# The output sums of an attention's last head group laid out anew over its slots, and wo's range maxima pinned into the filter's first loop

## The chip, the cores and the metric

The kernel runs on one core of a Trainium2 chip. The metric is the device time of one execution in microseconds (us), as the median of several runs; lower is better. Alongside it stands a profile: one execution recorded by the hardware, with the start and end of every instruction on each engine. PE is the matrix engine (TensorE), DVE the vector engine, ACT the scalar engine, POOL the general engine (GpSimd), SP the engine that issues the transfers (DMA). All times are in us unless ns stands beside them. L443 means line 443 of the kernel before.

## The reference, cut to what matters

Two layers, each an attention block and then a spectral filter, on x of 2048 x 1024 in float32:

```python
x = A_x
x = x + _A_ref(_layernorm(x, axis=-1), A_wqkv, A_wo)   # 32 heads of 32, softmax, output times wo
x = x + _B_ref(_layernorm(x, axis=-1), B_w_r, B_w_i)   # rfft2, times w, irfft2
x = x + _A_ref(_layernorm(x, axis=-1), A_wqkv, A_wo)
x = x + _B_ref(_layernorm(x, axis=-1), B_w_r, B_w_i)
return x
```

The end of `_A_ref` is what the change moves: the heads' outputs o (2048 x 1024), times wo (1024 x 1024), added to x.

## The kernel before

**Attention.** The 32 heads are worked in eight head groups of four (g = 0 to 7). A group runs over four chunks of 512 queries (c) and sixteen tiles of 128 keys (kt), so 64 steps u. A step computes the scores of one key tile for four heads (`S`, L558: twelve matmuls on a quarter of the array each) into two score buffers of two PSUM banks, and ACT turns each of them into p by an exponential (L562). Every second step PE multiplies the p of the two steps before with V (`PV`, L568), and DVE adds p into two running sums (`add`, L579 and L581, one add of 128 x 1024 for each buffer), from which the softmax's divisor comes at the end of a chunk (`fin`, L587 to L594); `out` (L600, L601) then makes the normalised head outputs as two float16 parts. There are three score buffers (`psS`), used in turn; L587's sums and the rests (below) take one of the same three.

**Slots.** After every odd step the order of PE's work, which is written out by hand (PE and ACT keep the order of the program in this part), has a slot for other matmuls: u // 2 counts them, 32 in a group. In groups 0 to 6 they hold the next group's projections. The output product is done in the slots at the end of group 6 and in those of group 7.

**The output product.** It goes by 12 tiles t of 128 rows (chunks 0 to 2, four tiles each); the last chunk's four tiles come after the slots, in the tail (`first`, `last`, `whole`). A tile has two halves of 512 columns. The heads' outputs of groups 0 to 6 are read back from DRAM by `load_o(c)` (L432 to L435, two loads of 896 KB), into one of two places that chunks c and c + 2 share; those of group 7 are still in SBUF (`olast`) but are ready only some steps into the next chunk. So a tile has a **part** (`wo_part`, groups 0 to 6: 21 matmuls for each half, into the only bank `x`, then one evacuation on DVE that adds the residual `xres`, L466) and a **rest** (`wo_rest` and `wo_last`, group 7: 6 matmuls into a score buffer, L443, then on DVE the evacuation of 1024 columns, L475, the statistics for the next layer norm, L477 and L498, and a store to y, L478). `wo_part` is a generator that yields after each matmul; a slot takes so many steps of it.

In the slots of group 7 a slot takes either 21 steps (one half's part) or one rest. Tiles 2 and 3 have their parts in group 6; the 20 halves of 0, 1, 4 to 11 follow in that order, and rests go into every fourth step from the point on at which olast is there. `load_o(2)` comes after tile 1, `load_o(3)` after tile 7.

**The planner.** On the engines whose order isn't written out (DVE, POOL and SP in attention, all engines elsewhere) the framework orders the instructions by its own simulation: of those that are ready by its clock, the first in the program goes first. An instruction with its data early can so be issued far ahead of where the program has it. Each engine then takes its instructions strictly in the order that the planner wrote. Buffers are handed on when the last reader is done.

**The tail and the filter.** After the slots PE does the last chunk's tiles; meanwhile DVE and ACT normalise and fold the first twelve (`fold_rests`, L513 on ACT, L146 and L147 on DVE), which needs the statistics of all twelve (`mvs`). The filter then starts with a loop of 33 turns (`t1`, `fa`: transposes L791, matmuls L800, ACT's copies L96 and L804, DVE's subtraction L805), and a second loop over 32 units of the spectrum, whose weights w are loaded by `loadw` (L834). In layer 0 alone the first loop also takes the greatest magnitude of wo, for a check of the inputs' range that is read at the end: every odd turn loads a sixteenth of wo (L780, three buffers), and from the third on reduces one that was loaded before (`absmax`, L784, L785), the last three in one turn. The buffers of the first loop are freed at its end, and their memory is used again for the second's.

Of the kernel before, what the change touches and what calls it, by code (L numbers as in the profile page):

```python
# [6 lines left out]
F32 = mybir.dt.float32  # L7
# [5 lines left out]
ALU = mybir.AluOpType  # L13
AX = mybir.AxisListType
# [156 lines left out]
def run(g):  # L171
    for _ in g:
        pass
# [96 lines left out]
def attention(nc, tc, layer, ap, xin, yd, wts, wo, cst, dram, flags):  # L270
# [8 lines left out]
    sq, on, on2, sm = ap.sq, ap.on, ap.on2, ap.sm  # L279
# [5 lines left out]
    def bank():  # L285

        if both:
            both.append(True)
            if len(both) % 2:
                return psO.tile([128, 512], F32, name="o")  # L290
        return psX.tile([128, 512], F32, name="x")
# [104 lines left out]
    def sums(ph):  # L396
        return 8 if ph[0] == "v" else 4

    def filler():
        run(prep(phases[0]))  # L400
        for i, ph in enumerate(phases):
            nxt = prep(phases[i + 1]) if i + 1 < len(phases) else iter(())
            for n in range(sums(ph)):
                yield from (v_tiles if ph[0] == "v" else qk_chunk)(ph, n)
                for _ in range(1 + (n > 0)):
                    next(nxt, None)
            run(nxt)
# [6 lines left out]
    def load_wo():  # L414
        st = []

        def load(i):
            if i < 16:
                s = sgp.tile([128, 512], F32, name="wst")
                nc.sync.dma_start(s, wo[i // 2 * 128:i // 2 * 128 + 128, i % 2 * 512:i % 2 * 512 + 512])  # L420
                st.append(s)
        load(0)
        load(1)
        for i in range(16):
            load(i + 2)
            d, sl = i // 2, slice(i % 2 * 512, i % 2 * 512 + 512)
            split(nc, wo_t[0][d // 4][:, d % 4, sl], wo_t[1][d // 4][:, d % 4, sl], st[i], SW)
            yield
# [3 lines left out]
    def load_o(c):  # L432
        osb[c] = xhl[:, 2 + c % 2]
        for i in range(2):
            nc.sync.dma_start(osb[c][:, i, 0:7], od[i, 0:7, :, c * 512:(c + 1) * 512].rearrange("g p n -> p g n"))  # L435

    def wo_mm(p, c, t, n, ds, start=True, stop=True):

        for d in ds:
            oh, ol = ((olast[c][:, i] if d == 7 else osb[c][:, i, d])[:, t * 128:t * 128 + 128] for i in range(2))  # L440
            wh, wl = (wo_t[i][d // 4][:, d % 4, n * 512:n * 512 + 512] for i in range(2))
            for i, (a, b) in enumerate(((oh, wh), (oh, wl), (ol, wh))):
                nc.tensor.matmul(p, a, b, start=start and d == ds[0] and i == 0, stop=stop and d == ds[-1] and i == 2)  # L443
                yield

    def xres(c, t):
        if c == 3:
            x = pp.tile([128, 1024], F32, name="xres", tag="p")
        else:
            x = wqp.tile([128, 1024], F32, name="xres", tag="wqk")  # L450
        r0 = c * 512 + t * 128
        nc.sync.dma_start(x, xin[r0:r0 + 128, :])
        return x

    def wo_part(c, t, dst):

        x = xres(c, t)
        for n in range(2):
            p = bank()
            m = wo_mm(p, c, t, n, range(7))  # L460
            for _ in range(20):
                next(m)
                yield
            run(m)
            sl = slice(n * 512, n * 512 + 512)
            nc.vector.scalar_tensor_tensor(dst[:, sl], p, 1.0 / (SO * SW), x[:, sl], op0=ALU.mult, op1=ALU.add)  # L466
            yield

    def wo_last(c, t, p, src, y, start):

        for n in range(2):
            run(wo_mm(p[:, n], c, t, n, (7,), start=start))
        st = sm.tile([128, 2, 6], F32, name="st")
        r0 = c * 512 + t * 128
        nc.vector.scalar_tensor_tensor(y, p.rearrange("p n c -> p (n c)"), 1.0 / (SO * SW), src, op0=ALU.mult, op1=ALU.add)  # L475
        for n in range(2):
            nc.vector.bn_stats(st[:, n], y[:, n * 512:n * 512 + 512])  # L477
        nc.sync.dma_start(yd[r0:r0 + 128, :], y)  # L478
        return st

    wo_dst = [ap.x[:, 10 + t if t in SPILL else t] for t in range(8)] + [None] * 2 + [ap.x[:, t] for t in (10, 11)]

    def wo_parts():
        load_o(0)
        load_o(1)
        for t in [2, 3, 0, 1] + list(range(4, 12)):
            if t == 8:
                two = wvp.tile([128, 2, 1024], F32, name="wv")
                wo_dst[8], wo_dst[9] = two[:, 0], two[:, 1]
            yield from wo_part(t // 4, t % 4, wo_dst[t])  # L490
            if t in (1, 7):
                load_o(t // 4 + 2)

    mvs = sm.tile([128, 24], F32, name="mvs")

    def wo_rest(t):
        p = psS.tile([128, 2, 512], F32, name="s")
        nc.vector.bn_aggr(mvs[:, 2 * t:2 * t + 2], wo_last(t // 4, t % 4, p, wo_dst[t], wo_dst[t], True))  # L498
# [107 lines left out]

    pend, done, late = [], [], []
    fill, lwo, wof = filler(), load_wo(), wo_parts()
    left, parts, rests = 16, 20, list(range(12))

    def slots(f, sums, n, steps):

# [12 lines left out]
    with tc.manual_schedule(engines={mybir.EngineType.PE, mybir.EngineType.Activation}):  # L625
        for g in range(NG):
            todo = sum(sums(ph) for ph in beside.get(g, []))
            sl = slots(fill, todo, 22 if g == NG - 2 else 32, 24)
            wsl = slots(wof, 4, 10, 21)
            for u in range(NCH * NKT):  # L630
                c, kt = divmod(u, NKT)
                S(g, c, kt)
                if kt % 2 == 0:
                    for w in pend:
                        PV(*w)
                    late = pend
                    pend = []
                for w in late[:1]:
                    add(*w)
                    if w[2] == NKT - 1:  # L640
                        fin(*w[:2])
                        done = [w[:2]]
                late = late[1:]
                if kt == 5 and done:
                    out(*done.pop())
                pend.append((g, c, kt))
                if kt % 2 == 0:
                    continue
                if todo:
                    todo = next(sl)  # L650
                elif g == NG - 2:
                    if left:
                        run(lwo)
                        left = 0
                    if next(wsl, None) is not None and u == NCH * NKT - 1:
                        run(wsl)
                elif g == NG - 1:
                    t = rests[0] if rests else 16
                    if (t // 4 < c - 1 or t // 4 == c - 1 and kt >= 7) and (kt % 4 == 3 or not parts):
                        wo_rest(rests.pop(0))  # L660
                    elif parts:
                        parts -= 1
                        for _ in range(21):
                            next(wof)
                if g == NG - 2 and todo < 4:
                    for _ in range(2):
                        if left > (8 if todo == 3 else 0):
                            next(lwo, None)
                            left -= 1
        for w in pend:  # L670
            PV(*w)
        for w in late + pend:
            add(*w)
        run(wof)
        for t in rests:
            wo_rest(t)
    with tc.manual_schedule(engines={mybir.EngineType.PE}):
        ps, xs, folds = [], [xres(3, t) for t in range(4)], fold_rests()

# [70 lines left out]
def spectral(nc, tc, ap, yd, xout, a, cst, fast, flags=None, nxt=None):  # L750
# [7 lines left out]
    sfx, parts = ("_", 2) if fast else ("", 1)  # L758
# [15 lines left out]
    wos = []  # L774

    def absmax(i):

        if flags is not None and 0 <= i < 16:
            s = p3.tile([128, 512], F32, name="wo")
            nc.sync.dma_start(s, a["wo"][(i // 2) * 128:(i // 2 + 1) * 128, (i % 2) * 512:(i % 2) * 512 + 512])  # L780
            wos.append(s)
        while len(wos) == 3 or (wos and i == 15):
            m = p3.tile([128, 1], F32, name="wom")
            nc.vector.tensor_reduce(m, wos.pop(0), axis=AX.X, op=ALU.max, apply_absolute_value=True)  # L784
            nc.vector.tensor_max(flags["w"], flags["w"], m)  # L785

    def t1(i):
# [22 lines left out]
    for i in range(33):  # L810
        cur = t1(i) if i < 32 else None
        if prev is not None:
            fa(i - 1, prev)
        prev = cur
        if i % 2:
            absmax(i // 2)
# [127 lines left out]
    for i in range(36):  # L944
# [8 lines left out]
        if i % 2 and i < 32:  # L953
            t = i // 2
# [44 lines left out]
    for i in range(17):  # L999
        cur = [t2(i, g) for g in range(2)] if i < 16 else None  # L1000
        if prev is not None:
# [5 lines left out]
            elif i % 2 == 0:  # L1007
                sl = slice(i * 64 - 128, i * 64)
# [228 lines left out]
```

## Time and profile before

| | |
|---|---|
| median of 3 runs | 3907.49 us (3906.37 to 3912.81) |
| span of the profiled execution | 3906.3 us |
| its own time beside the span | none is listed |
| PE busy | 3737.0 us (96%) |
| DVE busy | 3181.5 us (81%) |
| ACT busy | 2899.6 us (74%) |
| POOL busy | 637.5 us (16%) |
| chain of work that ended last, by engine | PE 75%, DVE 10%, issue 7%, ACT 4% |

The views that the prediction reads: busy time by stretch (a row is the stretch, its length, then the busy time and number of instructions of PE, its weight loads, DVE, ACT and POOL, the granted clock of PE, the DMA engines' share and their GB/s); waits (who waited for whom: total us, times, longest); and the instructions in order of time (start, duration, engine, line, operation, tiles out<-in, shapes, how many were merged, and in brackets how long the engine had been idle and what ended it). Instructions overlap a little at their ends, so start to start says more of the pace than the durations do.

### The profile page before, as it was taken

The numbers are of one execution on the slowest core, as the hardware profiler recorded it, in microseconds if no ns is written. First come the engines' busy times: TensorE is split into PE (matmuls) and PEld (weight loads), VectorE is DVE, ScalarE is ACT, GpSimd is POOL, SyncE is SP. The second block draws the span as 40 slices with busy tenths as digits, with TensorE's granted clock in tenths as the row PEclk, the third lists the DMA queues.
The fourth block names the chain that finished last, engine by engine and source line by source line (L and its number), as shares of the span: only waits on it lengthen the run. The fifth ranks groups of instructions, "written<-read, shape, count | busy, mean of one in ns | idle before, by whom it ended". The sixth has DMA issues, their size and how long they took to land.

```text
span 3906.3 us, 79627 instructions
## 1 busy us (share of the span) xinstructions
PE 3737.0 (96%) x32951; PEld 1642.5 (42%) x32951; DVE 3181.5 (81%) x3793; ACT 2899.6 (74%) x3567; POOL 637.5 (16%) x560
## 2 busy tenths in 40 slices
PE   6999999999999999989989999999999999999998
PEld 4322432342234233368853334333423432333788
DVE  6689899889998987966665998889899888788554
ACT  4577787888788865657855888888888887666686
POOL 1111011101110200014321221122121102000143
PEclk9999999999999999999999999999999999999999
DMA  8000000000000221134170000000000002111333
GB/s 203 15 12 23 12 12 17 18 12 17 15 23 7 71 71 64 64 139 142 62 176 12 15 23 12 12 18 22 10 18 12 23 12 90 52 68 66 146 97 105
DMA packets 165573, 194.07 MB, mean 50 GB/s; under 512 B 74960, under 2 KB 120656, under 8 KB 164176
## 3 DMA queue, kind: packets, MB, share of 16 engines
q1 hardware_dynamic: 164912, 188.82, 15.2%
q8 instruction: 260, 4.26, 0.4%
q14 instruction: 113, 0.93, 0.1%
q10 hardware_dynamic: 288, 0.07, 0.0%
HBM read 123.83 MB, written 48.23 MB: 44 GB/s over the span
## 4 chain that ended last, share of the span: by engine, by line
PE 75%; DVE 10%; issue 7%; ACT 4%; DMA 2%; POOL 2%; SPq 0%; DVEq 0%; ACTq 0%; POOLq 0%
PE o L568 21%; PE s L558 17%; PE x L340 13%; PE x L384 7%; PE x L443 6%; ACT p L562 2%; DVE R L581 2%; PE ps L862 2%; PE ps L800 1%; PE s L587 1%; DMA w<-in_w 1%; PE ps L791 1%; PE s L443 1%; PE ps L977 1%; PE o L384 1%
## 5 line engine op out<-in xcount | busy, mean ns | idle before, releaser
L562 ACT ACTIVATE p<-s,bias 128x1024 f32<-128x1024 f32 x2048 | 2169.0, 1111 | 589.9 <-PE s L558 578.4
L581 DVE TENSOR_TENSOR R<-R,p 128x1024 f32<-128x1024 f32 x1792 | 2146.8, 1251 | 148.3 <-ACT p L562 144.2
L568 PE MATMUL o<-p,R 128*32 128x512 f32 x8192 | 986.1, 599 | 0.0
L340 PE MATMUL x<-big,wqk 128*128 128x512 f16 x2880 | 685.6, 384 | 21.9 <-DVE R L168 8.1
L558 PEld LDWEIGHTS <-R 32*128 32x128 f16 x12288 | 232.5, 92 | 780.2 <-issue 664.6
L340 PEld LDWEIGHTS <-wqk 128*128 128x128 f16 x3072 | 277.9, 98 | 460.1 <-issue 167.5
L558 PE MATMUL s<-R 32*128 32x512 f16 x6144 | 432.5, 379 | 19.1 <-ACT p L562 15.6
L558 PE MATMUL s<-Q,R 32*128 32x512 f16 x6144 | 433.0, 378 | 11.9 <-ACT p L562 10.6
L568 PEld LDWEIGHTS o<-p,R 128*32 128x32 f32 x8192 | 213.9, 109 | 525.6 <-issue 525.0
L601 POOL TENSOR_TENSOR ohl<-zt,ohl 128x512 f16<-128x512 f32 x62 | 180.3, 2907 | 1473.6 <-ACT ohl L600 1473.6
L384 PEld LDWEIGHTS <-big 128*128 128x128 f16 x3072 | 295.0, 99 | 159.7 <-issue 79.1
L384 PE MATMUL x<-wv,big 128*128 128x256 f16 x2688 | 323.2, 277 | 40.6 <-DMA big<-hl 34.6
L579 DVE SCALAR_TENSOR_TENSOR R<-p 128x1024 f32<-128x1024 f32 x128 | 153.9, 1204 | 198.7 <-ACT p L562 198.4
L344 POOL TENSOR_TENSOR sq<-R 128x512 bf16<-128x512 f16 x96 | 144.5, 1505 | 693.8 <-ACT R L167 690.6
L443 PE MATMUL x<-big 128*128 128x512 f16 x1050 | 237.4, 380 | 0.0
L443 PEld LDWEIGHTS <-big 128*128 128x128 f16 x1344 | 126.3, 98 | 177.3 <-issue 33.9
L910 DVE TENSOR_TENSOR H<-G,H 128x512 f16<-128x512 f32 (+1 forms) x68 | 46.9, 690 | 104.7 <-ACT H L909 104.6
L862 PE MATMUL ps<-cbi,H 128*128 128x256 f16 (+1 forms) x792 | 99.2, 273 | 5.6 <-ACT H L909 3.3
L855 ACT COPY U<-ps 64x256 f32<-64x256 f32 (+1 forms) x272 | 97.0, 357 | 8.5 <-PE ps L862 3.3
L855 ACT COPY B<-ps 64x256 f32<-64x256 f32 (+1 forms) x272 | 97.0, 356 | 6.7 <-PE ps L862 3.2
L344 POOL TENSOR_TENSOR sq<-Q 128x512 bf16<-128x512 f16 x32 | 44.6, 1395 | 319.7 <-ACT Q L167 319.7
L862 PE MATMUL ps<-cb,big 128*128 128x256 f16 x780 | 96.4, 273 | 0.0
(429 smaller groups left out, 3017.1 us busy)
## 6 DMA issues: line engine op xcount, KB each, us to landing
wst<-in_wp SPq DMA_DIRECT2D x96, 256.0 KB, 3.0
R<-y SPq DMA_DIRECT2D x32, 512.0 KB, 5.4
w<-in_w SPq DMA_DIRECT2D x60, 256.0 KB, 2.6
od<-ohl SPq DMA_DIRECT2D x56, 256.0 KB, 2.4
big<-od SPq DMA_DIRECT2D x16, 896.0 KB, 6.6
y<-R SPq DMA_DIRECT2D x20, 512.0 KB, 2.7
R<-in_x SPq DMA_DIRECT2D x16, 512.0 KB, 5.6
wst<-in_wo SPq DMA_DIRECT2D x32, 256.0 KB, 2.9
```

The costliest lines, as they stand in the source:

```text
L340: nc.tensor.matmul(ps, a, b, start=d == 0 and i == 0, stop=d == 7 and i == 2)
L344: nc.gpsimd.tensor_tensor(nrm[ph][:, c], t[:, 0], t[:, 0], op=ALU.mult)
L384: nc.tensor.matmul(ps[:, j], l, r, start=d == 0 and i == 0, stop=d == 7 and i == 2)
L443: nc.tensor.matmul(p, a, b, start=start and d == ds[0] and i == 0, stop=stop and d == ds[-1] and i == 2)
L558: nc.tensor.matmul(s[h // 2][:, h % 2], K[g][r, a, kt * 128:kt * 128 + 128], Q[g][r, b, c * 512:c * 512 + 512], start=i == 0, stop=i == 2)
L562: nc.scalar.activation(p, s[hf], AF.Exp, bias=bias[g], scale=SCALE / (SQ * SQ))
L568: nc.tensor.matmul(O[g, c][32 * h:32 * h + 32], V[g][:, kt, 32 * h:32 * h + 32], P[g, c, kt, h // 2][:, h % 2], start=kt == 0, stop=kt == ...
L579: nc.vector.scalar_tensor_tensor(acc[hf], P[g, c, 0, hf], 1e-34, p, op0=ALU.add, op1=ALU.add)
L581: nc.vector.tensor_add(acc[hf], acc[hf], p)
L601: eng.tensor_tensor(t[:, 1], r, t[:, 0], op=ALU.subtract)
L855: nc.scalar.copy(ov[64 * r:64 * r + 64, a0:a0 + m, x], tl[64 * x:64 * x + 64, :m, r])
L862: nc.tensor.matmul(out, l, r, start=k == 0, stop=k == len(mm_) - 1)
```

## The change

Tiles 1 and 11 become whole: their two halves take all eight groups in `wo_part` (24 matmuls each), with the statistics and the store there, and have no rest. The order of the tiles is 2, 3 (group 6), then 0, 4, 5, 6, 7, 1, 8, 9, 10, 11; `load_o(3)` follows tile 7 and `load_o(2)` tile 1, directly before tile 8. A table says how many steps of the parts each of the 32 slots takes (21 in ten slots, 8 in six, 11 and 10 in turn in twelve, 12 in four), and another in which slot each of the ten rests comes: always after the slot's own steps. The tensor for the statistics, `mvs`, is allocated earlier. In `absmax` the reduction is pinned: it may not be ordered ahead of the DVE instruction that stands before it in the program.

```diff
-    def wo_part(c, t, dst):
+    mvs = sm.tile([128, 24], F32, name="mvs")
+
+    def wo_part(c, t, dst, nd):
 
         x = xres(c, t)
+        st = sm.tile([128, 2, 6], F32, name="st")
         for n in range(2):
             p = bank()
-            m = wo_mm(p, c, t, n, range(7))
-            for _ in range(20):
+            m = wo_mm(p, c, t, n, range(nd))
+            for _ in range(3 * nd - 1):
                 next(m)
                 yield
             run(m)
             sl = slice(n * 512, n * 512 + 512)
             nc.vector.scalar_tensor_tensor(dst[:, sl], p, 1.0 / (SO * SW), x[:, sl], op0=ALU.mult, op1=ALU.add)
+            if nd == 8:
+                nc.vector.bn_stats(st[:, n], dst[:, sl])
+                if n:
+                    r0 = c * 512 + t * 128
+                    nc.sync.dma_start(yd[r0:r0 + 128, :], dst)
+                    nc.vector.bn_aggr(mvs[:, 8 * c + 2 * t:8 * c + 2 * t + 2], st)
             yield
...
-        for t in [2, 3, 0, 1] + list(range(4, 12)):
+        for t in (2, 3, 0, 4, 5, 6, 7, 1, 8, 9, 10, 11):
...
-            yield from wo_part(t // 4, t % 4, wo_dst[t])
-            if t in (1, 7):
-                load_o(t // 4 + 2)
-
-    mvs = sm.tile([128, 24], F32, name="mvs")
+            yield from wo_part(t // 4, t % 4, wo_dst[t], 8 if t in (1, 11) else 7)
+            if t in (7, 1):
+                load_o(3 if t == 7 else 2)
...
-    left, parts, rests = 16, 20, list(range(12))
+    left, rests = 16, {}
+    share = [21] * 10 + [8] * 6 + [11, 10] * 6 + [12] * 4
+    for t, n in zip((0, 2, 3, 4, 5, 6, 7, 8, 9, 10), (11, 13, 15, 20, 22, 24, 26, 28, 29, 30)):
+        rests[n] = t
...
                 elif g == NG - 1:
-                    t = rests[0] if rests else 16
-                    if (t // 4 < c - 1 or t // 4 == c - 1 and kt >= 7) and (kt % 4 == 3 or not parts):
-                        wo_rest(rests.pop(0))
-                    elif parts:
-                        parts -= 1
-                        for _ in range(21):
-                            next(wof)
+                    for _ in range(share[u // 2]):
+                        next(wof)
+                    if u // 2 in rests:
+                        wo_rest(rests[u // 2])
...
         run(wof)
-        for t in rests:
-            wo_rest(t)
...
             m = p3.tile([128, 1], F32, name="wom")
-            nc.vector.tensor_reduce(m, wos.pop(0), axis=AX.X, op=ALU.max, apply_absolute_value=True)
+            tc.keep_in_program_order(nc.vector.tensor_reduce(m, wos.pop(0), axis=AX.X, op=ALU.max, apply_absolute_value=True))
             nc.vector.tensor_max(flags["w"], flags["w"], m)
```

## The prediction, made before the kernel was run

> **What bounds the kernel now.** I read the span first, then the busy time of each engine by stretch, then who waited for whom, then the instructions in order of time where a wait shows.
>
> ```profile
> span 3906.3 us, 79627 instructions
> ```
>
> The profiled execution has no time of its own beside this span; the three runs have a median of 3907.49, so the span stands 1.2 below it. I make the sum against the span and shift it by 1.2 at the end.
>
> The change works in two places: the last head group of each layer, and the passage from attention to the filter in layer 0. First the last head group of layer 1, the stretches of its second to fourth chunk (columns: length; busy time of PE, its weight loads, DVE, ACT, POOL; granted clock; DMA):
>
> ```profile
> 3425.70:3483.40 57.70, 56.25 (x451) 18.57 (x445) 44.56 (x48) 34.86 (x34) 1.82 (x1) 1.00 0.22 78
> 3483.40:3539.00 55.60, 53.67 (x438) 17.37 (x436) 50.20 (x56) 34.96 (x34) 1.92 (x1) 1.00 0.16 58
> 3539.00:3591.60 52.60, 50.66 (x419) 16.03 (x419) 48.60 (x55) 34.94 (x34) 1.92 (x1) 1.00 0.14 54
> ```
>
> PE is busy nearly throughout, DVE 143.4 of 165.9 us, ACT 104.8. So PE sets the pace, with DVE not far behind. All that PE waited for in this group is one row, and it is the same row in both layers:
>
> ```profile
> PE s L558 <- ACT p L562: 5.3, 11, 0.5
> ```
>
> Where it waits, in order of time:
>
> ```profile
> 3472.49 4.71 PE L443 MATMUL x<-big 128*128 128x512 f16 x21
> 3477.13 0.82 PE L558 MATMUL s<-Q,R 32*128 32x512 f16 x12
> 3477.89 1.92 PE L568 MATMUL o<-p,R 128*32 128x512 f32 x16
> 3479.74 0.83 PE L558 MATMUL s<-Q,R 32*128 32x512 f16 x12
> 3480.50 1.47 PE L443 MATMUL s<-big,ohl 128*128 128x512 f16 x6
> 3481.90 0.39 PE L558 MATMUL s<-Q,R 32*128 32x512 f16 x2
> 3482.77 0.82 PE L558 MATMUL s<-Q,R 32*128 32x512 f16 x10 [0.48 <-ACT p L562]
> 3483.53 1.92 PE L568 MATMUL o<-p,R 128*32 128x512 f32 x16
> 3485.38 0.83 PE L558 MATMUL s<-Q,R 32*128 32x512 f16 x12
> 3486.14 1.06 PE L587 MATMUL s<-R,ones 128*32 128x512 f32 x8
> ```
>
> The first four rows are a slot with a part of 21 matmuls, the next five a slot with a rest of 6. A slot is its output matmuls, then scores, PV, scores. From 3472.49 to 3480.50 it takes 8.01: the 21 matmuls 4.64 (0.221 each), the fixed work 3.37. A rest slot should take 3.37 + 6 x 0.221 = 4.70. It takes 5.64 (3480.50 to 3486.14), because the rest holds the third score buffer and the next scores need the buffer that ACT is still reading: two of twelve start, the other ten wait. The loss is 0.94, not the 0.48 of the idle column, since the two early matmuls are shown for longer than they work. Check on the second chunk: 8 slots x 3.37, 123 x 0.221, about 1.0 for the sums of L587 and 3 x 0.94 make 58.0; the row says 57.7.
>
> The Trainium skill, "Perfetto Trace Analysis", section Identifying the Most-Contended Engine, calls matmul occupancy no good measure of headroom, since PE is pipelined; by the idle column alone the term below would be 5.3 a layer, and the pitch of the slots sides with the page.
>
> Second, the passage. DVE in both layers (the 24 folds' start to the last normalisation), and the maxima of wo:
>
> ```profile
> L784 DVE TENSOR_REDUCE wom<-wo x16: 669/686/693, 1683.6 to 1709.7; 128x1 f32<-128x512 f32 x16
> ```
>
> ```profile
> 1660.49 0.21 DVE L498 BATCH_NORM_AGGREGATE mvs<-st 128x2 f32<-128x12 f32 x1
> ...
> 1711.25 0.48 DVE L716 TENSOR_SCALAR R<-R,r 128x512 f32<-128x512 f32 x1
> ```
>
> ```profile
> 3597.88 0.21 DVE L498 BATCH_NORM_AGGREGATE mvs<-st 128x2 f32<-128x12 f32 x1
> ...
> 3639.47 0.48 DVE L716 TENSOR_SCALAR R<-R,r 128x512 f32<-128x512 f32 x1
> ```
>
> The same work takes 50.76 in layer 0 and 41.59 in layer 1. The difference, 9.17, is what the maxima and their loads cost: the planner has hoisted them out of the filter's loop into the attention's end.
>
> **The change part by part.**
>
> *Rests behind other matmuls.* The matmuls stay 492 (8 tiles x 42, 2 x 48 and 10 rests x 6; before 20 x 21 and 12 x 6). After, a rest follows 8 to 12 others, so 14 to 18 matmuls, 3.1 to 4.0 us, lie between one slot's scores and the next, where ACT needs about 2.3 to clear both buffers (scores end at 3480.50, the wait ends at 3482.77):
>
> ```profile
> 3480.60 2.12 ACT L562 ACTIVATE p<-s,bias 128x1024 f32<-128x1024 f32 x2 [0.49 <-PE s L558]
> ```
>
> Slots of 8 without a rest leave 1.77, but there only one exponential has to be done. So all 11 waits go: 11 x 0.94 = 10.3 a layer, **20.7** in all. The ten slots of 21 that come first stay as they are. Allocating mvs earlier and st for every part issues no instruction.
>
> *What is late next: DVE.* A rest slot's work on DVE:
>
> ```profile
> 3468.10 1.22 DVE L581 TENSOR_TENSOR R<-R,p 128x1024 f32<-128x1024 f32 x1 [0.25 <-ACT p L562]
> 3469.24 1.22 DVE L475 SCALAR_TENSOR_TENSOR R<-s,R 128x1024 f32<-128x1024 f32 x1
> 3470.37 1.22 DVE L581 TENSOR_TENSOR R<-R,p 128x1024 f32<-128x1024 f32 x1
> 3471.51 1.28 DVE L477 BATCH_NORM_STATS2 st<-R 128x6 f32<-128x512 f32 x2
> 3472.70 1.21 DVE L581 TENSOR_TENSOR R<-R,p 128x1024 f32<-128x1024 f32 x1
> 3473.82 0.20 DVE L498 BATCH_NORM_AGGREGATE mvs<-st 128x2 f32<-128x12 f32 x1
> 3473.94 3.44 DVE L581 TENSOR_TENSOR R<-R,p 128x1024 f32<-128x1024 f32 x3
> 3477.30 0.69 DVE L466 SCALAR_TENSOR_TENSOR wv<-x,xres 128x512 f32<-128x512 f32 x1
> ```
>
> By start to start, four adds of 1.14, the rest's evacuation 1.13, its statistics 1.31: 7.0. PE needs 3.37 + 14 x 0.221 = 6.46 for a slot of 8 with a rest. In slots 10 to 15, three of them with rests, and with whole tile 1's two evacuations and statistics (about 0.6 each), DVE needs 37 against PE's 34.8, and the lag comes to 2 or 3. A rest's buffer must be free 2.6 after its last matmul (scores and PV of the next slot); without lag it is free at 2.1: these rows belong to the rest one period (8.01 + 5.64) before the quoted one, which ends at 3481.90 - 13.65 = 3468.25, and its evacuation is done at 3470.37. So the last rest of slots 10 to 15 stalls PE by about 1.2. Later slots have 10 to 12 others and DVE keeps up (7.0 of 7.1 to 7.4). I take **1.3 a layer**, bounds 0 and 3. The two whole tiles save a 1.13 evacuation each; that is in the 37.
>
> *load_o(2) moves to just ahead of its first use.* It waits for tile 1's last read of the buffer, five matmuls (1.1) into slot 15. Its loads, and how long each took to land:
>
> ```profile
> 3463.36 0.98 SPq L435 DMA_DIRECT2D big<-od x2
> ```
>
> ```profile
> big<-od SPq DMA_DIRECT2D x1, 896.0 KB, 4.8
> ```
>
> ```profile
> big<-od SPq DMA_DIRECT2D x2, 896.0 KB, 5.8
> ```
>
> The first takes 4.8, so with a median of 5.8 the second 6.8, issued half a microsecond later: it lands 8.4 into slot 15. Tile 8's third matmul needs it at 14 x 0.221 + 3.37 + 1.0 + 0.44 = 7.9. Cost **0.5 a layer**, bounds 0 (DVE's stall covers it) and 5 (rival A). Behind the waiting matmul stand the next scores, and so ACT and DVE. load_o(3) moves from this group's twelfth part to its tenth, far ahead of its use in the tail.
>
> *The tail.* PE works from the last slot to the end of attention without a wait in layer 1; tile 11's statistics come no later against it than the last rest's did. Nothing.
>
> *The maxima.* Pinned behind the filter loop's subtraction on DVE:
>
> ```profile
> 1760.41 0.69 DVE L805 TENSOR_TENSOR big<-ps,big 128x512 f16<-128x512 f32 x1 [0.78 <-ACT big L804]
> 1761.89 0.69 DVE L805 TENSOR_TENSOR big<-ps,big 128x512 f16<-128x512 f32 x1 [0.78 <-ACT big L804]
> ...
> 1767.32 0.69 DVE L837 TENSOR_REDUCE wbm<-w 128x1 f32<-128x512 f32 x1 [3.74 <-DMA w<-in_w]
> ```
>
> The loop's pitch is 1.48 with 0.78 idle; one maximum every second turn (0.69 and a small compare) fits. Three of wo's loads can still go ahead, each of the other thirteen goes out on SP after the maximum three before it, so six turns or 8.9 us ahead of its own maximum, behind the filter's constants. Layer 0's passage then takes layer 1's time: **-9.2**. But the last three come together, some 2.1 after the second-last subtraction, and the memory that holds wo's tiles is given to w, so w's first load, and the 1767.32 row behind it, may come up to 2.4 late; on SP only loads of y stand behind it, which the filter wants at its end. I take **+1.0**, bounds 0 (if that load is bound by others in flight) and 2.4.
>
> **Sum:** -20.7 + 2.6 + 1.0 - 9.2 + 1.0 = -25.3: span 3881, against the median **3882**. Best bounds: -20.7 - 9.2 = -29.9, 3877.6.
>
> **The rivals.**
>
> A. *Tile 8 waits longer.* If SP takes tile 1's output store first, which waits for DVE, load_o(2) issues at about 3.8 of slot 15 and PE waits 3 to 3.5. A restart can be slow:
>
> ```profile
> 3640.51 0.72 PE L791 MATMUL ps<-ident,R 128*128 128x128 f32 x2 [5.14 <-ACT R L715]
> ```
>
> ```profile
> 3640.50:3644.00 3.50, 3.49 (x15) 3.26 (x16) 0.00 (x0) 1.19 (x2) 0.00 (x0) 0.50 0.91 375
> ```
>
> After 5.14 idle the granted clock is 0.50 for 3.5 us, so 1.75 lost. Together 5 a layer: 3892. For it: SP is in order. Against: in the row above load_o issued as soon as its buffer was free. The Trainium skill, "TensorE: Matmul & The Clock Gate", Part 1, puts the point at an idle window of about 3.4 us; by that rule the forecast's 0.5 never trips it and rival A just may.
>
> B. *The pin moves the wait to SP.* If wo's loads, each waiting for a maximum three before, stand ahead of the filter's constants in SP's order, the constants go out after turn 30, 44 us into the loop. The first, 1.8 MB like load_o's pair, lands 7.3 later, one as large about as much after that, at 59; the second loop wants them from 47 to 49. So 10 come back: 3892. Against: the loop itself needs the first constant.
>
> C. *Slower: the rest's evacuation queues behind the next adds.* DVE takes its instructions in the planner's order. If that puts L475 behind the adds of the next step, which wait for its exponentials, the buffer is free at 0.8 (scores) + 2.1 (both exponentials) + 1.1 (the second's add) + 1.1 (itself) = 5.1, 2.5 after need. At 20 rests that is 50 against the other terms' 27.9: 3930. It decides from (27.9 + 7.8) / 20 = 1.8 a rest on; two adds that wait for nothing (2.1 + 2.3) stand on that edge. Against: L475 now runs between two adds. The Trainium skill, same page, section Architectural detail, calls VectorE's queue a strict first-in-first-out; by that rule a late evacuation can't be overtaken.
>
> **How the numbers follow.** A measurement of this kernel tells 0.2%, 7.8 us, from no change. Forecast 0.62 (3877 to 3888), A 0.10, B 0.10, both together or C at half of the rests 0.06 (3900 to 3915), C 0.08, below 3876 0.04. Range 3876 to 3894 holds the first three. Faster 0.62 + 0.10 + 0.10 + 0.04 = 0.86, within 0.06, slower 0.08.
>
> **What would show it.** Right: no PE wait for ACT at L558 in the last groups; their last three chunks together 157 instead of 166; L784 alternating with L805; layer 0's passage at 41.6. Wrong: PE waiting for DVE at L558, for a DMA at L443, L805 waiting for wo, or w landing over 2 later against the last L805. If DVE bounds slots 10 to 31 and not only 10 to 15, the first term is mis-sized.

## The result, and the profile after

The changed kernel takes 3899.59 us (median of 8 runs, 3898.46 to 3902.33); eight runs of the kernel before give 3910.44 (3906.37 to 3917.37). The ratio is 0.9972, 95% interval 0.9962 to 0.9982: 11 us faster where 25 were forecast, and above the range. The profiled execution of the changed kernel has a span 8.2 us below that of before:

```profile
span 3898.1 us, 79628 instructions
```

The change moves the line numbers: the scores L558 are now L565, a part's evacuation L466 is L469, a rest's evacuation L475 is L484 and its store L478 is L487; L474 is the store of a whole tile, and L443 stays. The filter's lines grow by 5. The second to fourth chunk of layer 1's last head group, in the same columns as before (length; PE, its weight loads, DVE, ACT, POOL; granted clock; DMA):

```profile
3422.40:3475.30 52.90, 52.26 (x440) 17.11 (x441) 44.71 (x47) 34.82 (x35) 1.83 (x1) 1.00 0.24 85
3475.30:3532.20 56.90, 51.46 (x428) 16.15 (x429) 47.86 (x54) 34.92 (x35) 1.83 (x1) 0.97 0.23 80
3532.20:3585.60 53.40, 53.40 (x435) 17.77 (x434) 50.40 (x59) 34.92 (x34) 2.36 (x1) 1.00 0.18 66
```

Together 163.2, against 165.9 before and 157 forecast. The second chunk is 4.8 shorter. The third is 1.3 longer although PE works 2.2 less in it, and it is the only one whose clock is below 1.00. What PE waited for in layer 1, from this group to the filter:

```profile
PE ps L796 <- ACT R L720: 5.1, 1, 5.1
PE x L443 <- DMA big<-od: 4.9, 1, 4.9
PE s L565 <- DVE R L484: 1.1, 2, 0.6
```

The first row is the passage's old wait. The row of eleven waits for ACT is gone; two rows are new, one for a load and one for DVE. Layer 0 has the same two, the load's 4.3 long, and on SP the same order as shown below (load, two stores, load). PE in order of time at the place of both (in the brackets the idle time and what ended it):

```profile
3475.18 1.92 PE L575 MATMUL o<-p,R 128*32 128x512 f32 x16
3477.66 0.83 PE L565 MATMUL s<-Q,R 32*128 32x512 f16 x12 [0.55 <-DVE R L484]
3478.41 1.07 PE L594 MATMUL s<-R,ones 128*32 128x512 f32 x8
3479.41 0.61 PE L443 MATMUL x<-big 128*128 128x512 f16 x2
3484.90 3.80 PE L443 MATMUL x<-big 128*128 128x512 f16 x9 [4.88 <-DMA big<-od]
3488.64 0.83 PE L565 MATMUL s<-Q,R 32*128 32x512 f16 x12
```

Tile 8 starts: its first two matmuls run, the third waits 4.88 for `load_o(2)`. After that nine matmuls take 3.80, where nine at 0.221 take 1.99. The granted clock in just that stretch (same columns as above) is 0.55:

```profile
3484.90:3488.70 3.80, 3.80 (x13) 1.24 (x17) 0.00 (x0) 0.00 (x0) 0.00 (x0) 0.55 0.01 5
```

The wait and the slow restart come to 4.88 + 1.81 = 6.7. Why the load was late, SP's queue shows (time at which the transfer was handed out):

```profile
3472.36 0.37 SPq L435 DMA_DIRECT2D big<-od  x1
3476.50 0.32 SPq L474 DMA_DIRECT2D y<-R  x1
3477.63 0.32 SPq L487 DMA_DIRECT2D y<-R  x1
3478.05 0.40 SPq L435 DMA_DIRECT2D big<-od  x1
```

`load_o(2)` is two loads. The first goes out at 3472.36; between it and the second stand two stores of y, and each waits for DVE:

```profile
3467.84 8.03 DVE L588 TENSOR_TENSOR R<-R,p 128x1024 f32<-128x1024 f32 x7
3475.79 0.68 DVE L469 SCALAR_TENSOR_TENSOR R<-x,xres 128x512 f32<-128x512 f32 x1
3476.39 1.21 DVE L484 SCALAR_TENSOR_TENSOR R<-s,R 128x1024 f32<-128x1024 f32 x1
```

Tile 1's evacuation ends at 3476.47 and its store goes out 0.03 later; tile 3's rest ends at 3477.60, its store 0.03 later. The second load follows at 3478.05, 5.7 after the first, and the wait of PE ends at 3484.90, 6.85 after that. DVE's lag thus costs PE little on its own (0.55 at 3477.66), and through SP a whole load.

In layer 0 the maxima have left the passage (first statistics to last normalisation, layer 0 and then layer 1):

```profile
1657.25 0.21 DVE L475 BATCH_NORM_AGGREGATE mvs<-st 128x2 f32<-128x12 f32 x1
...
1702.25 0.48 DVE L721 TENSOR_SCALAR R<-R,r 128x512 f32<-128x512 f32 x1
...
3589.71 0.21 DVE L475 BATCH_NORM_AGGREGATE mvs<-st 128x2 f32<-128x12 f32 x1
...
3634.71 0.48 DVE L721 TENSOR_SCALAR R<-R,r 128x512 f32<-128x512 f32 x1
```

45.00 in both layers. (Before, layer 1 had 41.59. The first row is now tile 11's statistics as a whole tile, which come earlier, and the last comes 1.3 later after the exponentials' end, since tile 11's slot holds 12 matmuls where a rest of 6 was; so only the equality tells something.) At the end of the filter's loop in layer 0, DVE:

```profile
1753.21 0.68 DVE L810 TENSOR_TENSOR big<-ps,big 128x512 f16<-128x512 f32 x1
...
1753.88 0.68 DVE L789 TENSOR_REDUCE wom<-wo 128x1 f32<-128x512 f32 x1
...
1755.21 0.69 DVE L789 TENSOR_REDUCE wom<-wo 128x1 f32<-128x512 f32 x1 [0.47 <-DMA wo<-in_wo]
...
1759.77 0.69 DVE L842 TENSOR_REDUCE wbm<-w 128x1 f32<-128x512 f32 x1 [3.42 <-DMA w<-in_w]
```

The last two maxima come after the last subtraction, and w's first maximum 6.56 after it. Before, that subtraction stood at 1762.88 and w's maximum, as quoted in the prediction, at 1767.32, so 4.44:

```profile
1762.88 0.69 DVE L805 TENSOR_TENSOR big<-ps,big 128x512 f16<-128x512 f32 x1 [0.30 <-ACT big L804]
```

PE there, after and then before (first matmul of the second loop, and its first with `cbi`, the inverse's):

```profile
1752.19 2.78 PE L867 MATMUL ps<-cb,big 128*128 128x256 f16 x24
1756.97 0.49 PE L899 MATMUL ps<-cc,B 128*128 128x128 f32 x2 [2.00 <-ACT B L860]
...
1765.80 0.39 PE L867 MATMUL ps<-cbi,H 128*128 128x256 f16 x2 [1.40 <-ACT H L914]
```

```profile
1762.06 2.78 PE L862 MATMUL ps<-cb,big 128*128 128x256 f16 x24
...
1772.05 0.39 PE L862 MATMUL ps<-cbi,H 128*128 128x256 f16 x2 [1.57 <-ACT H L909]
```

13.61 against 9.99, so 3.6 more. Some 2.1 of it come with a wait of 2.00 that before does not have: for ACT's copies into B. The other 1.5 are PE's pace after it: over the 3.4 from 1757.80 on the granted clock is 0.52. The run with the pin alone (below) has the same wait, 1.90 long, then a clock of 1.00, and its stretch takes 12.13, 2.1 more than before.

**Where the time went**, from these stretches. Layer 1, from its second chunk to the last normalisation, takes 212.3 where it took 213.8: 1.5 won. Layer 0 takes 212.2 for 223.0: 10.7 won, 9.2 more than layer 1, which is the maxima. Less 3.6 at the second loop that leaves 8.6; the spans differ by 8.2. That the two lie so close is in part luck, since stretches that no edit touches moved as well between the two profiles: up to layer 0's last group by +1.7, from the second loop of layer 0 to layer 1's last group by +3.0, behind layer 1's passage by -3.4.

### The profile page after: what moved, and what is told of

It reads as the page before. It is cut to its first block, busy times and chain, and to the rows that moved or that the text cites. A ratio compares the mean times of both kernels' runs of the same rounds, so it can differ in the third digit from the quotient of the medians.

```text
span 3898.1 us, 79628 instructions
## 1 busy us (share of the span) xinstructions
PE 3737.5 (96%) x32951; PEld 1643.1 (42%) x32951; DVE 3178.1 (82%) x3789; ACT 2901.1 (74%) x3567; POOL 639.7 (16%) x560
## 4 chain that ended last, share of the span: by engine, by line
PE 42%; DVE 6%; issue 3%; ACT 2%; POOL 2%; DMA 1%; SPq 0%; DVEq 0%; ACTq 0%; POOLq 0%
PE o L575 10%; PE s L565 8%; PE x L340 6%; PE x L384 4%; PE x L443 3%; PE ps L867 2%; PE ps L805 1%; PE s L443 1%; DVE R L588 1%; PE ps L796 1%; ACT p L569 1%; PE ps L982 1%; PE ps L936 1%; PE ps L899 1%; PE ps L970 1%
## 5 line engine op out<-in xcount | busy, mean ns | idle before, releaser
L565 PEld LDWEIGHTS <-R 32*128 32x128 f16 x12288 | 230.8, 92 | 771.1 <-issue 655.7
L565 PE MATMUL s<-R 32*128 32x512 f16 x6144 | 432.7, 379 | 21.8 <-ACT p L569 18.4
L575 PEld LDWEIGHTS o<-p,R 128*32 128x32 f32 x8192 | 213.8, 109 | 525.1 <-issue 525.1
L565 PE MATMUL s<-Q,R 32*128 32x512 f16 x6144 | 425.3, 378 | 4.2 <-DVE R L484 2.3
L443 PE MATMUL x<-big 128*128 128x512 f16 x1050 | 245.5, 384 | 9.2 <-DMA big<-od 9.1
L443 PEld LDWEIGHTS <-big 128*128 128x128 f16 x1344 | 125.0, 98 | 192.4 <-issue 46.4
```

The costliest lines, as they stand in the source:

```text
L565: nc.tensor.matmul(s[h // 2][:, h % 2], K[g][r, a, kt * 128:kt * 128 + 128], Q[g][r, b, c * 512:c * 512 + 512], start=i == 0, stop=i == 2)
L575: nc.tensor.matmul(O[g, c][32 * h:32 * h + 32], V[g][:, kt, 32 * h:32 * h + 32], P[g, c, kt, h // 2][:, h % 2], start=kt == 0, stop=kt == ...
```

## The experiments

The theory after the result: of the missing 14 us, some 12 are the wait for `load_o(2)` with its slow restart (6.7 a layer for 0.5), and some 2 are the filter's second loop starting late because the last maxima hold memory that w and B are to have. The rival: the gain of the slots themselves was overrated (DVE has too little room in slots 10 to 31, or the whole tiles cost more than they save), and the load's wait only covers DVE time that would be waited for anyway.

**Each half alone.** Before, with the pin only:

```diff
-            nc.vector.tensor_reduce(m, wos.pop(0), axis=AX.X, op=ALU.max, apply_absolute_value=True)
+            tc.keep_in_program_order(nc.vector.tensor_reduce(m, wos.pop(0), axis=AX.X, op=ALU.max, apply_absolute_value=True))
```

> The kernel before with the pinned maxima alone. Theory (the slots' gain was eaten by the wait for load_o(2); the pin kept its gain): layer 0's passage falls by 9.2, the second loop starts about 3 later, so 6 below the kernel before (ratio about 0.9985), no PE wait of over 1 in the last head group but the old 11. Rival (the pin is what disappointed, the slots gave the 8 to 11 measured): within 2 of the kernel before.

Measured: 3906.63 against 3911.1, ratio 0.9984 (0.9975 to 0.9993). The waits of PE in the last group and DVE's passage in layer 0:

```profile
PE s L558 <- ACT p L562: 5.3, 11, 0.5
```

```profile
1668.92 0.21 DVE L498 BATCH_NORM_AGGREGATE mvs<-st 128x2 f32<-128x12 f32 x1
...
1710.50 0.48 DVE L716 TENSOR_SCALAR R<-R,r 128x512 f32<-128x512 f32 x1
```

The passage takes 41.58 for 50.76: the whole 9.18 is the pin's, and the slots' waits are untouched by it. The ratio gives 6.3 (2.7 to 9.8), as the theory has it and outside the rival's 2; some of the 9.18 is given back in the filter, where w stands later here too, 6.4 after the last subtraction.

The changed kernel without the pin:

```diff
-            tc.keep_in_program_order(nc.vector.tensor_reduce(m, wos.pop(0), axis=AX.X, op=ALU.max, apply_absolute_value=True))
+            nc.vector.tensor_reduce(m, wos.pop(0), axis=AX.X, op=ALU.max, apply_absolute_value=True)
```

> The changed kernel without the pin. Theory: the second to fourth chunk and the tail together give 1.5 a layer, so 3 below the kernel before (0.9992), with PE waiting 4 to 5 for big<-od in each layer. Rival (the slots gave the whole difference): 8 to 11 below.

Measured: 3905.07, ratio 0.9986 (0.9976 to 0.9995): 5.5 (2 to 9.4). PE in layer 1's last group:

```profile
PE x L443 <- DMA big<-od: 4.8, 1, 4.8
```

The load's wait belongs to the slots, not to the pin; in layer 0 it is 3.7. The time decides nothing between the theory's 3 and the rival's 8 to 11, since its interval reaches into both. The passage in layer 0 takes 52.5 here, against 45.0 with the pin, so behind the new slots the pin is worth 7.5 there and not 9.2. The halves' 6.3 and 5.5 make 11.8, the whole change by its ratio 10.9. The slots alone were forecast at 17 (20.7 less 2.6 and 1.0), so the failure lies mostly there.

**The load first.** The changed kernel, with `load_o(2)` called right behind the last matmul that reads its buffer, so ahead of tile 1's evacuation, store and the next rest in the program:

```diff
-            for _ in range(3 * nd - 1):
+            for i in range(3 * nd - 1):
                 next(m)
+                if n and i == 20 and (c, t) == (0, 1):
+                    load_o(2)
                 yield
...
-            if t in (7, 1):
-                load_o(3 if t == 7 else 2)
+            if t == 7:
+                load_o(3)
```

> The changed kernel with load_o(2) called straight after tile 1's last matmul that reads the shared buffer, so both loads stand ahead of the two output stores on SP. Theory (the second load is late because it stands behind two stores that wait for DVE): it is issued about 5 earlier, PE's wait for big<-od falls from 4.9 to under 1, the granted clock stays 1.00, the third chunk takes 50 instead of 56.9, and the time falls by 12 to about 3888. Rival 1 (two loads of 896 KB are too slow whenever they go out): the wait stays above 3 and the time falls by under 4. Rival 2 (DVE's lag is the bound there): the wait for DVE at L565 grows by what the load gives back, and the time falls by under 4.

Measured: 3887.06, ratio 0.9937 (0.9924 to 0.9951). SP's queue, PE at tile 8, and the third chunk (the edit adds 2 to the line numbers behind it):

```profile
3464.25 0.98 SPq L435 DMA_DIRECT2D big<-od  x2
3468.39 0.33 SPq L476 DMA_DIRECT2D y<-R  x1
3469.53 0.33 SPq L489 DMA_DIRECT2D y<-R  x1
```

```profile
3471.31 2.55 PE L443 MATMUL x<-big 128*128 128x512 f16 x11
```

```profile
3467.20:3517.30 50.10, 49.54 (x428) 15.82 (x428) 47.62 (x54) 34.87 (x34) 1.83 (x1) 1.00 0.25 91
```

Both loads go out together, the stores follow, the eleven matmuls of tile 8 run in one piece, and the chunk takes 50.1 for 56.9, at clock 1.00. Here the load's price stands alone: 6.6 in layer 0 and 6.7 in layer 1, from the second chunk to the last normalisation. The rival's half about the cover falls: DVE's waits stay at 1.2 a layer, as in the changed kernel.

**No whole tiles.** The changed kernel with twelve rests again, spread behind other matmuls, and the tiles' old order, in which `load_o(2)` is long ahead of its use:

```diff
-        for t in (2, 3, 0, 4, 5, 6, 7, 1, 8, 9, 10, 11):
+        for t in (2, 3, 0, 1, 4, 5, 6, 7, 8, 9, 10, 11):
...
-            yield from wo_part(t // 4, t % 4, wo_dst[t], 8 if t in (1, 11) else 7)
+            yield from wo_part(t // 4, t % 4, wo_dst[t], 7)
...
-    share = [21] * 10 + [8] * 6 + [11, 10] * 6 + [12] * 4
-    for t, n in zip((0, 2, 3, 4, 5, 6, 7, 8, 9, 10), (11, 13, 15, 20, 22, 24, 26, 28, 29, 30)):
+    share = [21] * 10 + [7] * 6 + [11, 10] * 8
+    for t, n in zip(range(12), (11, 13, 15, 17, 20, 22, 24, 26, 28, 29, 30, 31)):
```

> The changed kernel with the old order of tiles and no whole tile: 12 rests, each behind other matmuls, and load_o(2) four tiles ahead of its use. Theory: all 11 waits at the scores go and no load is waited for, 10.3 a layer less up to 2 for DVE, which evacuates two tiles more: 157 or less for the last three chunks of a layer, and with the pin 22 to 24 below the kernel before (about 3887). Rival (DVE bounds the slots as soon as PE's waits go): PE waits for DVE at the scores for over 5 a layer, and the time is within 4 of the changed kernel.

Measured: 3891.63, ratio 0.9945 (0.9931 to 0.9958). The third chunk of layer 1, and PE's wait for DVE:

```profile
3469.40:3521.30 51.90, 50.91 (x434) 16.50 (x438) 50.56 (x56) 34.91 (x34) 1.51 (x1) 1.00 0.26 93
```

```profile
PE s L565 <- DVE R L484: 1.8, 2, 1.0
```

No wait for a load. The last three chunks take 156.2, as expected (157 or less), and the time is 21.5 below before by the ratio, where 22 to 24 were expected. From the second chunk to the last normalisation a layer takes 206.2, against 213.8 before and 205.6 with whole tiles and the load first. The rival's other half falls as well: putting rests behind other matmuls is nearly the whole gain of the slots, the whole tiles add about 0.6 a layer, the same in both layers, and the order that they came with brought the load's wait.

**The maxima earlier.** The changed kernel, with two maxima in every three turns from the seventh on, so that all sixteen are done with the loop:

```diff
-        if i % 2:
-            absmax(i // 2)
+        if i > 5 and i % 3 < 2:
+            absmax(2 * (i // 3 - 2) + i % 3)
```

> The changed kernel with two maxima in three turns of the filter loop from its sixth on, so that the last three end four turns before the loop. Theory (the last three maxima hold the memory that the second loop's w and B get): w's first load goes out with the last matmul again and lands 4.4 behind the last subtraction, not 6.5, PE's wait for ACT's copies into B (2.0) goes, and the time falls by 2 to 3 against the changed kernel (about 3897). Rival (what lies behind w's load hides it): w lands earlier, the time stays within 1 of the changed kernel.

Measured: 3894.75 against 3910.8, ratio 0.9965 (0.9953 to 0.9977), an interval that overlaps the changed kernel's. What the times leave open, the trace shows. DVE's last subtraction and w's first maximum:

```profile
1751.52 0.69 DVE L810 TENSOR_TENSOR big<-ps,big 128x512 f16<-128x512 f32 x1
1756.03 0.69 DVE L842 TENSOR_REDUCE wbm<-w 128x1 f32<-128x512 f32 x1 [3.83 <-DMA w<-in_w]
```

PE at the second loop's start:

```profile
1750.70 2.78 PE L867 MATMUL ps<-cb,big 128*128 128x256 f16 x24
...
1760.76 0.39 PE L867 MATMUL ps<-cbi,H 128*128 128x256 f16 x2 [1.65 <-ACT H L914]
```

4.51 and 10.06, as before the change (4.44 and 9.99). The wait for B is gone too: w's load and ACT's copies into B were late because the last maxima were. (In the changed kernel the first of these copies had waited 3.20 for the last maximum.)

**Both.** The edits of "the load first" and "the maxima earlier" together:

> load_o(2) straight after its last reader and the maxima early, together. Theory: the two gains add, 12 and 2 to 3 below the changed kernel, about 3885 (ratio to the kernel before about 0.993). Rival for the second part: the time of the run with the load alone, 3887.

Measured: 3880.21, ratio 0.9923 (0.991 to 0.9937), the lowest median of all. Layer 1's third chunk takes 50.2 at a granted clock of 1.00. That is 30 us below before, by the ratio 25 to 35: what the prediction had asked of the change as it stood. For the second part the times don't decide against the rival, since the interval overlaps that of the load alone; that w and B come in time again rests on the trace.

**The first rests apart.** As "both", with the rests of tiles 2 and 3 in slots 14 and 17 in place of 13 and 15, to be rid of the 1.2 that PE waits for DVE:

```diff
-    for t, n in zip((0, 2, 3, 4, 5, 6, 7, 8, 9, 10), (11, 13, 15, 20, 22, 24, 26, 28, 29, 30)):
+    for t, n in zip((0, 2, 3, 4, 5, 6, 7, 8, 9, 10), (11, 14, 17, 20, 22, 24, 26, 28, 29, 30)):
```

> As e6_first_early, with tile 2's and 3's rests at slots 14 and 17 instead of 13 and 15. Theory (DVE falls behind in slots 10 to 15, which hold three rests and a whole tile): PE's two waits for L484's evacuation, 1.2 a layer, go, and the time falls by 2.4 against e6_first_early. Rival (DVE's lag only moves on with the rest): the waits stay at 1 to 1.5 a layer, at another slot.

Measured: 3885.35, ratio 0.9931 (0.9918 to 0.9945). The gain expected did not come. The waits for DVE are gone, and PE at tile 8 shows what took their place:

```profile
3468.69 0.60 PE L443 MATMUL x<-big 128*128 128x512 f16 x2
3470.61 2.12 PE L443 MATMUL x<-big 128*128 128x512 f16 x9 [1.32 <-DMA big<-od]
```

PE now gets to tile 8 sooner than the load does, though this goes out at once. In "both" the third matmul was due 7.5 after the first load's issue; here it is due after 5.7, and the load is there after 7.1. Of the difference, 1.3 are the six matmuls of tile 3's rest, which had stood in slot 15 between the load and its use, and 0.6 the wait for DVE. So the rest had covered the load more than DVE had. With the wait for DVE alone gone, the third matmul would be due after 6.9, about 0.2 ahead of the load: an estimate from these rows, which fits the prediction's bound of nothing (DVE's stall covers it) and isn't tested by itself. The restart after 1.32 idle is at full speed: nine matmuls in 2.12.

**A whole tile far from its load.** The changed kernel with the maxima earlier, tiles 7 and 11 whole, and tiles 8 and 9 ahead of 7, so that both loads lie far ahead of their uses:

```diff
-        for t in (2, 3, 0, 4, 5, 6, 7, 1, 8, 9, 10, 11):
+        for t in (2, 3, 0, 1, 4, 5, 6, 8, 9, 7, 10, 11):
...
-            yield from wo_part(t // 4, t % 4, wo_dst[t], 8 if t in (1, 11) else 7)
+            yield from wo_part(t // 4, t % 4, wo_dst[t], 8 if t in (7, 11) else 7)
...
-    share = [21] * 10 + [8] * 6 + [11, 10] * 6 + [12] * 4
-    for t, n in zip((0, 2, 3, 4, 5, 6, 7, 8, 9, 10), (11, 13, 15, 20, 22, 24, 26, 28, 29, 30)):
+    share = [21] * 10 + [7] * 6 + [11, 10] * 2 + [12] * 4 + [11, 10] * 2 + [12] * 4
+    for t, n in zip((0, 1, 2, 3, 4, 5, 6, 8, 9, 10), (11, 14, 16, 18, 20, 22, 24, 28, 29, 30)):
```

> Tile 7 is whole instead of tile 1, tile 1 keeps its old place, so that load_o(2) has twelve slots to land; rests spread, maxima early. Theory (only the distance of the load counted): no wait for big<-od, PE's waits in the last head group under 1 a layer, and the time that of e8_rests_apart within 2, about 3883. Rival (something else about the old order of the tiles helped e3): over 5 slower than e6_first_early.

Measured: 3886.83, ratio 0.9937 (0.9923 to 0.995). All that PE waits for in layer 1's last group:

```profile
PE s L565 <- DVE R L484: 0.4, 1, 0.4
```

A layer from its second chunk to the last normalisation takes 205.5 here, 205.6 in "both" and 205.9 with the rests apart. By its medians this run meets the theory's condition (within 2 of the rests apart) and the rival's (over 5 above "both") at once. The three can't be ranked: their intervals overlap, and a stretch of layer 0 that no edit touches, from the last sums (L587 before) of its first head group to those of its seventh, alone varies from 1104.9 to 1113.3 between the profiles; it is 1108.7 in "both", 1112.3 with the rests apart and 1112.9 here.

## Why the prediction was wrong

The direction was right and the size was not: 11 us came of 25. Point by point, by the prediction's steps:

- **The eleven waits** (20.7 in all). The step held, and its size was a little too large. No wait for ACT at the scores is left. A slot of 11 with a rest of 6, PE in order of time:

```profile
3509.14 2.55 PE L443 MATMUL x<-big 128*128 128x512 f16 x11
3511.52 1.46 PE L443 MATMUL s<-big,ohl 128*128 128x512 f16 x6
3512.91 0.83 PE L565 MATMUL s<-Q,R 32*128 32x512 f16 x12
...
3516.28 2.33 PE L443 MATMUL x<-big 128*128 128x512 f16 x10
```

  It takes 7.14; 3.37 + 17 x 0.221 is 7.13. With the load first, a layer gains 8.2 (213.8 to 205.6) with 1.2 of waits for DVE in it, so the waits brought 9.4 a layer, 0.9 less than 10.3. Most of that lies in the 0.94 for one wait. It was the slot's 5.64 less 4.70, with 6 x 0.221 = 1.33 for the rest. But from a rest to the next scores it is 1.40 in the prediction's own rows (3480.50 to 3481.90), and 1.39 here, where nothing waits. So a wait cost 0.87, which is the 0.48 of the idle column and the 0.39 of the two early matmuls, and eleven cost 9.6.
- **DVE** (1.3 a layer). Right in its sum: 1.1 to 1.2, at the rests of slots 13 and 15 with about 0.6 each, not at the last alone. In part that is luck: the lag of 2 to 3 less the slack of 0.5 (2.6 less 2.1) would have made 1.5 to 2.5 of it, and the prediction gives no working for its 1.2.
- **load_o(2)** (0.5 a layer, bounds 0 and 5). This is the step that failed: "in the row above load_o issued as soon as its buffer was free". That row is of a kernel in which no store stood beside the load. The first of the two loads did so again; the second did not. It stood 5.7 on SP behind two stores which waited for DVE's evacuations. Measured in layer 1: 6.7, 4.9 of wait and 1.8 of half clock. Over two layers that is 12.4 too little, most of what is missing (14 between the medians, 17 between the spans). It is rival A, which the prediction held at 0.10 and priced at 5 (by its own terms that comes to 3891, not 3892). Its form differs: not all of `load_o(2)` behind one store, but its second half behind two. That a long wait is followed by half clock it had right. The Trainium skill, "TensorE: Matmul & The Clock Gate", Part 1, gives an idle window of about 3.4 us as the point. The traces agree with it on the long and the short waits (clock 0.55 after 4.88 idle, nine matmuls at full speed after 1.32) and not in between: half clock followed a wait of 2.00 in the second loop and of 2.08 in the rows at the end of this document.
- **The maxima** (9.2). Right: 9.18 by the pin alone, 9.2 as the layers' difference. (Taken from the kernel that has the slots, it is 7.5.)
- **w's first load** (1.0, bounds 0 and 2.4). The mechanism was right and w came 2.1 late, within the bounds. But w was not all that waited: ACT's copies into B waited for the same memory, PE for them, and the second loop's start lost 2.1 with the pin alone and, with a half clock behind the wait, 3.6 in the changed kernel. The term was too small by 1.1 to 2.6.
- **Rivals B and C** did not come. No wait for wo or for the filter's constants shows in the loop (the last maximum alone waits 0.47 for its own load); the rest's evacuation does come late behind adds, but no wait of PE for it is over 0.6.

With the measured terms, the eleven waits at 9.4 a layer, the sum is -18.8 + 2.3 + 13.4 - 9.2 + 3.6 = -8.7, against 8.2 between the spans and 11 between the medians (7 to 15 by the ratio's interval).

The prediction did ask what stands ahead of the load on SP, in rival A, but put it aside for a row of the kernel before. What stands there after the change, and what that waits for, was in the code: the store of tile 1, which the whole tile had just put there, and that of tile 3's rest in slot 15. And DVE's lag of 2 to 3, which the prediction itself had worked out, is how late the first of them is: tile 1's matmuls end at 3473.03, its evacuation starts at 3475.79.

**What stays open.** Why the planner put the stores between the two loads and not ahead of both or behind; a load in one piece was not tried, so whether the split matters is not shown. That the stores are the cause is shown only with the program's order changed (the load first), not by taking the stores away.

## What to carry to other kernels

Where a change gives an engine's queue a transfer shortly before its data are needed, list what stands ahead of it in that queue and what each of these waits for; a store that waits for a lagging engine passes the lag on to every load behind it. Call a load in the program right behind the last reader of its buffer, ahead of the stores of the same step. And count what stands between a load's issue and its use as the load's cover: when six matmuls and a wait were moved away from there, the load's own wait came up in their place.

## What the runs showed of the hardware that was not expected

A wait of PE can have a second price. After the six waits for `load_o(2)` of 3.69 to 5.17, in three traces, nine matmuls took 3.41 to 4.02 (3.80 at a granted clock of 0.55 in the one shown), after the two of 1.32 and 1.41 they took 2.12. So the same load, given to the queue 5.7 later, cost not the lateness alone (4.9) but a third more. At about 2 its length doesn't tell whether the price is charged. The same twelve matmuls of layer 0, behind the same wait and far from any edit, in the kernel before and then with the pin alone:

```profile
984.86 2.75 PE L340 MATMUL x<-big,wqk 128*128 128x512 f16 x12 [2.08 <-DVE Q L168]
```

```profile
987.30 4.42 PE L340 MATMUL x<-big,wqk 128*128 128x512 f16 x12 [2.08 <-DVE Q L168]
```

The granted clock over the 3.4 from 987.70 on is 0.56 in the second. So one such event costs about 1.7, and profiles can differ by several of them where nothing was changed: the 8.4 between these two in the stretch of layer 0 named above would be five (an estimate). What decides between the two at such a wait no run here shows.
